# GpSimd asks for pair 1's q, k and v before it sets up constants

## The chip, the cores and the metric

The kernel runs on one core of a Trainium2 chip. A core has engines that run side by side and wait for one another through semaphores: TensorE (PE, with its weight loads shown as PEld), VectorE (DVE), ScalarE (ACT), GpSimd (POOL) and SyncE (SP). Loads and stores are asked for by an engine and carried out by 16 DMA engines. The metric is the device time of one execution in microseconds (us); less is better. Before the change it was 261.1 us, the median of 3 runs (260.87 to 262.47).

## The reference

Linear attention without a softmax, RMS norm over the head dimension, then two matrix products with a gate between them:

```python
kv = np.einsum('bhsd,bhse->bhde', k, v)
out = np.einsum('bhsd,bhde->bhse', q, kv)
rms = np.sqrt(np.mean(out * out, axis=-1, keepdims=True) + 1e-06)
x = out / rms * g_norm          # 8 batches, 8 heads, 576 rows, 64 wide
# x transposed to (8 * 576, 512)
h = x @ w_in                    # 512 -> 2048
g = h * (1.0 / (1.0 + np.exp(-1.702 * h)))
return g @ w_out                # 2048 -> 512
```

All inputs are float32; the kernel computes in float16 with float32 sums.

## The kernel before

Work goes batch by batch: attention of a batch gives `xT` (the transposed, normed rows), and then come the two products with the gate (`Hidden`, `SevenIn`, `Seven`). Attention of the next batch is woven into the products of the present one by lists of steps written out by hand; each engine carries out its instructions in the order in which the program names them. From batch 1 on, that order keeps PE in dense work. Batch 0 has nothing to be woven into and stands alone at the start; the change lies there.

The eight heads of a batch are four **pairs**, numbered 0 to 3. Batch 0 does for each pair `c`:

- `q(c)` (L408): twelve transposes on PE with the identity `ident`, then a copy to `qT` on DVE (L418).
- `kv(c)` (L399): twelve small products of k and v (L249), then on DVE (L402) the copy to `kvb`, multiplied by `ones2`, a 128 x 128 matrix of two 64 x 64 blocks of ones, so that the two heads of a pair don't mix.
- `out(c)` (L282): the product of `kvb` and `qT`, then Square on ACT (L300).
- `ss(c)` (L357): a product with `ones2` that adds up the squares, then the reciprocal root on ACT (L359).
- `apply(c)` (L367): on DVE, the output times the root and `g_col`, written to `xT`.

The pairs are interleaved from L851 on. The order on PE is: twelve `busy` products (512 columns wide, on a zeroed tile, whose results nobody reads), `q(0)`, two more `busy`, `kv(0)`, two small products for `g_col`, two `busy`, `out(0)`, `q(1)`, `kv(1)`, `ss(0)`, `out(1)`, `q(2)`, `kv(2)`, `ss(1)`, `out(2)`, `q(3)`, `kv(3)`, `ss(2)`, the first two products with `w_in` (L451), `out(3)`, further products with `w_in`, and among them `ss(3)`; the products that need `apply(3)` end this part. On DVE, `apply(0)` stands behind the `kvb` copy of pair 2, `apply(1)` between the `qT` copy and the `kvb` copy of pair 3.

Loads of batch 0 come on two queues. SyncE asks for pair 0's k, q and v (L152) in float32, into the staging tile `qf`; DVE and ACT cast them to float16 (L833 to L835). GpSimd asks for q, k and v of pairs 1, 2 and 3 (`early_load`, L90), nine loads, which convert to float16 on the way. The weights follow on GpSimd's queue: seven loads of `w_in` (L171), then `w_out` (L196) and batch 1's q, k, v. Eight semaphores take turns for GpSimd's loads: from the ninth load on, each issue waits for the landing of the load eight places before it.

Before its first load, GpSimd sets up constants. DVE zeroes `ident` (L155) and `kvb[1]` (L156), which the `busy` products read. GpSimd then writes the ones onto the diagonal of `ident` with a select (L157), and fills `ones2` by three memsets (L166 to L168):

```python
nc.gpsimd.memset(ones2, 0.0)
nc.gpsimd.memset(ones2[0:D, 0:D], 1.0)
nc.gpsimd.memset(ones2[D:P, D:P], 1.0)
...
for c in range(1, NPAIR):
    for n in "qkv":
        early_load(n, 0, c, c + 1)
```

Of the kernel before, what the change touches and what calls it, by code (L numbers as in the profile page):

```python
# [9 lines left out]
ALU = mybir.AluOpType  # L10
AFT = mybir.ActivationFunctionType

P = 128
# [3 lines left out]
def kernel(  # L17
# [10 lines left out]
    nc = tc.nc  # L28

    B, H, S, D = q.shape  # L30
# [39 lines left out]
    ident = const.tile([P, P], F16)  # L70
    ones2 = const.tile([P, P], F16)
# [14 lines left out]
    def early_src(n, b, c0, c1):  # L86
        return srcs[n][b, 2 * c0 : 2 * c1].rearrange("h (p j) d -> p h (j d)", j=NJ)

    def early_load(n, b, c0, c1):
        nc.gpsimd.dma_start(  # L90
            out=raw[n][0:PE_, c0:c1, :].rearrange("p c (l x) -> p (c l) x", l=2),
            in_=early_src(n, b, c0, c1),
        )
# [52 lines left out]
    for n in "kqv":  # L146
# [7 lines left out]
    nc.scalar.dma_start(out=g_row, in_=g_norm.unsqueeze(0))  # L154
    nc.vector.memset(ident, 0.0)  # L155
    nc.vector.memset(kvb[1], 0.0)  # L156
    nc.gpsimd.affine_select(  # L157
        out=ident,
        in_=ident,
        compare_op=ALU.not_equal,  # L160
        fill=1.0,
        base=0,
        pattern=[[-1, P]],
        channel_multiplier=1,
    )
    nc.gpsimd.memset(ones2, 0.0)  # L166
    nc.gpsimd.memset(ones2[0:D, 0:D], 1.0)
    nc.gpsimd.memset(ones2[D:P, D:P], 1.0)  # L168

    def load_w_in(f0, f1, k0=0, k1=KO):  # L170
        nc.gpsimd.dma_start(  # L171
            out=w_in_sb[:, k0:k1, f0 * P : f1 * P],
            in_=moe_w_in[k0 * P : k1 * P, f0 * P : f1 * P].rearrange(
                "(ko ki) f -> ki ko f", ki=P
            ),
        )

    for c in range(1, NPAIR):
        for n in "qkv":
            early_load(n, 0, c, c + 1)  # L180
    load_w_in(0, 4, 0, 1)
    load_w_in(0, 4, 1, 2)
    load_w_in(0, 4, 2, KO)
# [887 lines left out]
```

## Time and profile before

| | |
|---|---|
| time, median of 3 runs | 261.1 us (260.87 to 262.47) |
| the profiled execution's own time | 260.98 us |
| its span in the profile | 259.2 us |
| PE busy | 251.8 us (97% of the span) |
| DVE busy | 194.7 us (75%) |
| ACT busy | 174.9 us (67%) |
| POOL busy | 53.6 us (21%) |

Times in the profile count from the start of the span. A timeline row gives start, duration, engine, line, operation, what it writes and reads, how many instructions are merged into it, and in brackets how long the engine sat idle before it and what ended that. "issue" there means that no cause is shown. A row with DMA on POOL or on SPq (SyncE's queue) is the issue of a load, not its transfer. In the view of DMA queues, q0 is GpSimd's queue and q1 SyncE's; a row gives packets, MB, and the time that the packets took as a share of 16 engines over the stretch, which passes 100% where packets of one engine overlap. The chain that ended last is followed back from the last instruction, at each step to whatever released it.

### The profile page before, as it was taken

The numbers are of one execution on the slowest core, as the hardware profiler recorded it, in microseconds if no ns is written. First come the engines' busy times: TensorE is split into PE (matmuls) and PEld (weight loads), VectorE is DVE, ScalarE is ACT, GpSimd is POOL, SyncE is SP. The second block draws the span as 40 slices with busy tenths as digits, with TensorE's granted clock in tenths as the row PEclk, the third lists the DMA queues.
The fourth block names the chain that finished last, engine by engine and source line by source line (L and its number), as shares of the span: only waits on it lengthen the run. The fifth ranks groups of instructions, "written<-read, shape, count | busy, mean of one in ns | idle before, by whom it ended". The sixth has DMA issues, their size and how long they took to land.

```text
span 259.2 us, 6157 instructions
## 1 busy us (share of the span) xinstructions
PE 251.8 (97%) x2500; PEld 206.3 (80%) x2500; DVE 194.7 (75%) x351; ACT 174.9 (67%) x315; POOL 53.6 (21%) x81
## 2 busy tenths in 40 slices
PE   8799999999999999999999999999999999999993
PEld 3444554788888988898889988988899888888882
DVE  1565676899968986898689958995899587557842
ACT  3477725988649964996499648974897569737820
POOL 8862245116034002500160017000000000000001
PEclk9999999999999999999999999999999999999999
DMA  7999999999999946994699799966500710021005
GB/s 174 198 202 206 204 204 196 228 188 146 201 144 193 198 78 163 153 214 71 159 105 230 102 143 157 219 82 158 154 1 12 160 73 3 0 97 68 3 0 162
DMA packets 68558, 35.31 MB, mean 136 GB/s; under 512 B 37874, under 2 KB 65778, under 8 KB 68402
## 3 DMA queue, kind: packets, MB, share of 16 engines
q0 software_dynamic: 37520, 18.17, 54.3%
q1 hardware_dynamic: 30688, 16.36, 27.5%
q8 instruction: 19, 0.31, 0.5%
q10 hardware_dynamic: 322, 0.39, 0.4%
q14 instruction: 9, 0.07, 0.1%
HBM read 36.70 MB, written 9.44 MB: 178 GB/s over the span
## 4 chain that ended last, share of the span: by engine, by line
PE 93%; POOL 2%; DMA 2%; DVE 1%; ACT 0%; issue 0%
PE h L558 38%; PE o L680 38%; PE o L794 5%; PE hT L451 5%; DMA vbuf<-in_v_dram 2%; PE outR L309 2%; PE kvp L237 2%; PE ss L357 1%; POOL qraw L90 1%; POOL kraw L90 1%; POOL vbuf L90 0%; PE kvp L249 0%; PE outT L282 0%; PE q L432 0%; DVE xT L367 0%; PE outT L286 0%
## 5 line engine op out<-in xcount | busy, mean ns | idle before, releaser
L538 ACT ACTIVATE gT<-h 128x512 f16<-128x512 f32 x96 | 52.8, 604 | 5.4 <-PE h L558 5.3
L558 PEld LDWEIGHTS <-ws 128*128 128x128 f16 x512 | 50.1, 98 | 5.8
L680 PEld LDWEIGHTS <-gS 128*128 128x128 f16 x512 | 49.7, 98 | 5.7
L558 PE MATMUL h<-xS,ws 128*128 128x256 f16 x384 | 52.2, 273 | 0.0
L680 PE MATMUL o<-tw,gS 128*128 128x256 f16 x384 | 46.3, 273 | 0.0
L558 PEld LDWEIGHTS <-w_in_sb 128*128 128x128 f16 x384 | 37.1, 98 | 4.7
L680 PEld LDWEIGHTS <-gT 128*128 128x128 f16 x384 | 37.0, 98 | 4.0
L680 PE MATMUL o<-w_out_sb,gT 128*128 128x256 f16 x256 | 33.5, 273 | 0.0
L558 PE MATMUL h<-xT,w_in_sb 128*128 128x256 f16 x224 | 31.9, 273 | 0.0
L655 DVE TENSOR_TENSOR osb<-o,qf 128x512 f32<-128x512 f32 (+1 forms) x25 | 16.7, 668 | 15.1 <-PE o L680 12.3
L572 DVE TENSOR_TENSOR h<-h,s 128x512 f32<-128x512 f32 x32 | 22.2, 697 | 6.8 <-PE h L558 5.5
L574 DVE TENSOR_TENSOR s<-h,s 128x512 f32<-128x512 f32 x32 | 22.1, 691 | 4.1 <-PE h L558 3.3
L114 POOL DMA_DIRECT2D kraw<-in_k_dram x7 | 6.0, 853 | 91.6 <-PE kvp L237 87.2
L610 DVE TENSOR_TENSOR gS<-gT 128x512 f16<-128x512 f16 (+2 forms) x32 | 21.7, 684 | 0.6 <-ACT gT L538 0.6
L538 ACT ACTIVATE gT<-s 128x512 f16<-128x512 f32 x32 | 19.8, 628 | 2.6 <-DVE s L574 2.6
L359 ACT ACTIVATE rs<-ss,eps_t 128x512 f32<-128x512 f32 (+1 forms) x16 | 9.2, 582 | 16.6 <-PE ss L357 16.5
L713 POOL DMA_DIRECT2D out_dram<-osb x2 | 1.1, 562 | 92.4 <-DVE osb L655 92.4
L558 PE MATMUL h<-xS,w_in_sb 128*128 128x256 f16 x128 | 18.9, 273 | 0.0
L966 ACT ACT_TABLE_LOAD x14 | 18.0, 1283 | 0.2
L508 ACT COPY h<-h 128x512 f32<-128x512 f32 x27 | 15.7, 585 | 2.1 <-PE h L558 2.0
L558 PE MATMUL h<-xT,ws 128*128 128x256 f16 x112 | 16.8, 273 | 0.0
L794 PE MATMUL o<-w_out_sb,gT 128*128 128x512 f16 x64 | 16.6, 380 | 0.0
(100 smaller groups left out, 367.8 us busy)
## 6 DMA issues: line engine op xcount, KB each, us to landing
out_dram<-osb SPq DMA_DIRECT2D x10, 512.0 KB, 3.1
kraw<-in_k_dram POOLq DMA_DIRECT2D x5, 512.0 KB, 7.8
vbuf<-in_v_dram POOLq DMA_DIRECT2D x5, 512.0 KB, 11.5
qraw<-in_q_dram POOLq DMA_DIRECT2D x3, 512.0 KB, 13.4
qbuf<-in_q_dram POOLq DMA_DIRECT2D x3, 512.0 KB, 12.7
out_dram<-osb SPq DMA_DIRECT2D x6, 192.0 KB, 6.1
w_in_sb<-in_moe_w_in_dram POOLq DMA_DIRECT2D x2, 512.0 KB, 10.5
w_out_sb<-in_moe_w_out_dram POOLq DMA_DIRECT2D x2, 512.0 KB, 15.1
```

The lines of the kernel that those rows point to most:

```text
L359: nc.scalar.activation(rs[:, 0:n], t[:, 0:n], AFT.Abs_reciprocal_sqrt, bias=eps_t, scale=1.0 / D)
L451: nc.tensor.matmul(self.h[fo], w_in_sb[:, ko, fo * P : (fo + 1) * P], self.x[:, ko], start=(ko == 0), stop=(ko == KO - 1),)
L508: (nc.vector.tensor_copy if engine == "D" else nc.scalar.copy)(to, src)
L538: nc.scalar.activation(self.gT[:, to, n * TH : (n + 1) * TH], src, AFT.Gelu_apprx_sigmoid)
L558: nc.tensor.matmul(bank[name][:, a], w, x, start=(p in (1, 5) and a == 0 and k == 0), stop=(k == KH - 1), skip_group_check=True,)
L572: nc.vector.tensor_add(bank["z"], bank["x"], self.s5)
L574: nc.vector.tensor_add(self.s5, bank["x"], self.s5)
L610: op(s[:, n, lo], a, b)
L655: nc.vector.tensor_add(o, ps, self.kept[with_][:, m])
L680: nc.tensor.matmul(o, a, w, start=(p in (1, 2, 5) and i == 0 and (mo == 0 or split)), stop=(i == HF - 1), skip_group_check=True,)
L794: nc.tensor.matmul(os[mo], gT[:, fo, mo * P : (mo + 1) * P], w_out_sb[:, fo, :], start=(fo == 0), stop=(fo == FO - 1),)
L966: u2.setdefault(i, []).append(lambda: f(*args))
```

## The change

The select on `ident` moves behind pair 1's three loads in GpSimd's program, and the three memsets of `ones2` go from GpSimd to DVE, behind the memset of `kvb[1]`. DVE's instructions are three more and GpSimd's three fewer; the order of everything else is as before on all engines. Nearly all lines behind the changed place stand one line further down in the new kernel (the copy to `kvb` is L403 there instead of L402); the issue of the `w_in` loads is L162 instead of L171 and keeps its place in the order.

```diff
     nc.vector.memset(ident, 0.0)
     nc.vector.memset(kvb[1], 0.0)
-    nc.gpsimd.affine_select(
-        out=ident,
-        in_=ident,
-        compare_op=ALU.not_equal,
-        fill=1.0,
-        base=0,
-        pattern=[[-1, P]],
-        channel_multiplier=1,
-    )
-    nc.gpsimd.memset(ones2, 0.0)
-    nc.gpsimd.memset(ones2[0:D, 0:D], 1.0)
-    nc.gpsimd.memset(ones2[D:P, D:P], 1.0)
+    nc.vector.memset(ones2, 0.0)
+    nc.vector.memset(ones2[0:D, 0:D], 1.0)
+    nc.vector.memset(ones2[D:P, D:P], 1.0)
...
     for c in range(1, NPAIR):
         for n in "qkv":
             early_load(n, 0, c, c + 1)
+        if c == 1:
+            nc.gpsimd.affine_select(
+                out=ident,
+                in_=ident,
+                compare_op=ALU.not_equal,
+                fill=1.0,
+                base=0,
+                pattern=[[-1, P]],
+                channel_multiplier=1,
+            )
```

## The prediction

> **What bounds the kernel now.** I read the busy shares first, then the stretches on either side of 17.15 us, then the chain that ended last, and last the timeline of the first 18 us.
>
> ```profile
> span 259.2 us, 6157 instructions
> PE 251.8 (97%) x2500; PEld 206.3 (80%) x2500; DVE 194.7 (75%) x351; ACT 174.9 (67%) x315; POOL 53.6 (21%) x81
> ```
>
> ```profile
> 17.15:254.95 237.80, 237.78 (x2364) 199.95 (x2363) 187.08 (x331) 167.03 (x305) 38.93 (x53) 1.00 0.81 132
> ```
>
> The second fence is the view by stretches (length, then PE, PEld, DVE, ACT, POOL, then the clock). From 17.15 us on, PE is busy 237.78 of 237.80 us: it waits for nothing. So whatever moves PE's start into that stretch moves the end by the same amount, and nothing after 17.15 us can be won by earlier loads. The profiled execution took 260.98 us, 1.78 us more than its span; the median of the runs shown is 261.1, that is 0.12 higher.
>
> The change lies in the first microseconds. The chain of waits names a load in front of that stretch:
>
> ```profile
> 7.34 5.59 DMA vbuf<-in_v_dram
> ...
> 13.06 0.38 PE kv L249 x12
> ...
> 17.15 4.48 PE hT L451 x20
> ```
>
> This is pair 3's v, the last of the nine loads that GpSimd asks for at L90. It lands at 12.93 (7.34 + 5.59) and PE's `kv(3)` starts at 13.06. The timelines of PE, DVE, GpSimd and SyncE's queue show what stands around it (start, duration, engine, line; in brackets the idle time ahead and its releaser):
>
> ```profile
> 7.60 0.38 PE L249 MATMUL kv<-vbuf,kraw 96*64 96x64 f16 x12 [0.63 <-DVE vbuf L835]
> ...
> 11.95 0.45 PE L412 MATMUL q<-ident,qraw 96*64 96x96 f16 x12
> 13.06 0.38 PE L249 MATMUL kv<-vbuf,kraw 96*64 96x64 f16 x12 [0.67 <-DMA vbuf<-in_v_dram]
> ...
> 13.64 0.61 PE L451 MATMUL hT<-xT,w_in_sb 128*128 128x512 f16 x2
> 14.09 0.38 PE L282 MATMUL outT<-qT,kvb 128*128 128x512 f16 x1
> ```
>
> ```profile
> 6.91 0.64 DVE L835 CAST vbuf<-qf 96x768 f16<-96x768 f32 x1 [2.37 <-DMA qf<-in_v_dram]
> ...
> 12.43 0.46 DVE L418 COPY qT<-q 128x576 f16<-128x576 f16 x1 [0.21 <-PE q L412]
> 12.81 0.74 DVE L367 SCALAR_TENSOR_TENSOR xT<-outT,g_col,rs 128x512 f16<-128x512 f32 x1
> 13.48 0.29 DVE L402 TENSOR_TENSOR kvb<-kv,ones 128x128 f16<-128x128 f32 x1
> ```
>
> ```profile
> 1.02 0.29 POOL L157 TENSOR_SCALAR_AFFINE_SELECT ident<-ident 128x128 f16<-128x128 f16 x1 [0.56 <-DVE ident L155]
> 1.26 0.20 POOL L166 MEMSET ones<- 128x128 f16 x1
> ...
> 1.70 0.15 POOL L168 MEMSET ones<- 64x64 f16 x1
> 1.79 0.78 POOL L90 DMA_DIRECT2D qraw<-in_q_dram  x1
> ```
>
> ```profile
> 0.76 0.41 SPq L152 DMA_DIRECT2D qf<-in_k_dram  x1
> 1.22 0.43 SPq L152 DMA_DIRECT2D qf<-in_q_dram  x1
> 1.70 0.45 SPq L152 DMA_DIRECT2D qf<-in_v_dram  x1
> ```
>
> There are two gates. At 7.60 PE starts `kv(0)`, 0.63 us idle, released by the cast of pair 0's v, which SyncE's queue brought. From there to 12.40 (11.95 + 0.45) runs a chain of latencies through PE, DVE and ACT. At 13.06 comes the second gate, 0.67 us idle, released by GpSimd's last load. But behind it DVE isn't free either: it is in `apply(1)` (L367) from 12.81 to 13.55, and the copy of `kv(3)` (L402) starts at 13.48, as that ends. Were the load earlier, the product behind `kv(3)` would wait for DVE instead of memory.
>
> **The change part by part.**
>
> *GpSimd's work ahead of its first load.* It loses the select and three memsets, which end at 1.85 (1.70 + 0.15). SyncE's first issue stands at 0.76, so the engines are free by then and the first issue moves from 1.79 to about 0.8: 1.0 us earlier. Pair 1's three issues follow; the select (0.29) now stands behind them, so pairs 2 and 3 are asked for about 0.7 earlier. The order of the loads is the same, and no wait on a landing moves to another load. Whatever the last load gains by this is bounded by the queue, not by its issue:
>
> ```profile
> vbuf<-in_v_dram POOLq DMA_DIRECT2D x3, 144.0 KB, 5.4
> ```
>
> Columns: how many, size of one, median us from issue to landing. Nine issues in the 5.55 us from 1.79 to 7.34 are 0.69 apart, and each waits 5.4 for its landing: about eight stand in line. The first lands near 7.2 (1.79 + 5.4), the ninth at 12.93, so one leaves the line each 0.72 us. Bringing requests forward to a line that is already full lands nothing earlier unless the line itself starts earlier.
>
> *Identity and ones.* PE needs `ident` at `q(0)`, which follows twelve warming matmuls; the select would end near 3.4 (0.8, three issues at 0.78 as the row at 1.79 has it, and 0.29). The three memsets on DVE cost at most about 0.5 together by GpSimd's own times (the longest quoted is 0.20), and stand ahead of nothing before the first cast near 4 us; the first reader of `ones2` is L402 after 8 us. The matmuls that warm PE wait only for `kvb[1]`, set before them. Cost: nothing; without that cover, DVE's 0.5 would delay the first cast.
>
> *What the earlier line meets.* Pair 0's k, q, v come on SyncE's queue at the same time; these are the last two:
>
> ```profile
> qf<-in_q_dram SPq DMA_DIRECT2D x1, 288.0 KB, 3.8
> qf<-in_v_dram SPq DMA_DIRECT2D x1, 288.0 KB, 5.2
> ```
>
> The packets by queue (q1 SyncE's, q0 GpSimd's), in 3.5 to 4.5, 4.5 to 5.0, 5.5 to 6.5 and 7.0 to 8.0 us, one fence each:
>
> ```profile
> q1 hardware_dynamic: 173, 0.24, 106.0%
> ```
>
> ```profile
> q1 hardware_dynamic: 75, 0.11, 91.9%
> q0 software_dynamic: 5, 0.00, 14.9%
> ```
>
> ```profile
> q0 software_dynamic: 255, 0.18, 120.1%
> q1 hardware_dynamic: 23, 0.03, 9.9%
> ```
>
> ```profile
> q0 software_dynamic: 276, 0.20, 132.4%
> ```
>
> Alone, SyncE's queue moves 173 packets a us, 10.8 on each of 16 engines: 92 ns each. Alone, GpSimd's moves 276: 58 ns each. GpSimd's first data move between 4.5 and 5.0, 2.7 us or more after the issue at 1.79. Between 5.5 and 6.5 the last 23 packets of SyncE's queue come through among 255 of GpSimd's, and pair 0's v lands only at 6.9 (1.70 + 5.2), 1.9 after q (1.22 + 3.8 = 5.0), though most of its packets were through by 5.5. An engine that serves both in turn gives SyncE's queue one packet per 150 ns (92 + 58).
>
> If GpSimd's data begin 1.0 us earlier, then in that us an engine moves 6.7 of SyncE's packets instead of 10.8. The 4.1 left over come through at 150 ns each: pair 0's v lands **0.62 us later**, at 7.53. Below lies nothing (if GpSimd's data wait until SyncE's queue runs dry), above 1.35 (if they begin 2.2 us earlier: the rival below). I take 0.62, since the mixed stretch in 5.5 to 6.5 is the nearest row.
>
> The Trainium skill's page "DMA: Bandwidth & Descriptors" (section Queues, rings and completion order) says that each DMA engine goes round its queues in turn, a packet block at a time; it speaks against asking early beside a load that is needed first. The mixed 5.5 to 6.5 agrees that neither queue has precedence. With strict halves, a us of earlier sharing would cost v 1.0 us rather than 0.62, and the sum would be 0.4 higher.
>
> *The path.* `kv(0)` moves from 7.60 to 8.22. The chain to the end of `q(3)` carries this along, 12.40 to 13.02; so `kv(3)` finds its v there, and starts at 13.06 as before. The 0.67 of idle time is used up, not won. But DVE carries 0.62 too: its copy at 12.43 goes to 13.05, `apply(1)` ends at 14.17, and the copy of `kv(3)` runs 14.10 to 14.39. `out(3)` can follow at 14.39 instead of 14.09. Before, it could have started at 13.77 (13.48 + 0.29) and stood behind the two products of 13.64; that slack, 0.32, is all that takes up some of the delay. After `out(3)` come Square, `ss(3)`, the root, `apply(3)` and the product at 17.15, one waiting for the other.
>
> Sum: 0.62 − 0.32 = **+0.30 us**, so 260.98 + 0.30 = 261.28 against the profiled run, 261.40 against the median. I give 261.3. A measurement of this kernel can tell about 1%, 2.6 us, from no change: this is well inside.
>
> **The rivals.**
>
> *Nothing moves.* GpSimd's data began at 4.5 to 5.0 just as SyncE's queue ran out; if that was the cause, v still lands at 6.9 and the time is 261.0 to 261.1. For it: only 5 packets before 5.0. Against it: once they came, they went beside SyncE's rather than behind.
>
> *The gain arrives.* If the DMA engines do more with both queues in line (75 + 5 packets in half a us before, 255 + 23 in a whole us after), the ninth load and the first weights land a little earlier. One us at 278 instead of 173 packets would be 105 packets, or 0.38 us at 276 a us. If v of pair 0 isn't late, `kv(3)` starts at 12.68 (13.06 − 0.38), yet `out(3)` still waits for DVE's copy (13.77): the gain is 0.32 at most, 260.7 to 260.9. This is the faster side, and it needs pair 0's v to land no later than 6.9 all the same.
>
> *A longer overlap.* The lag from issue to data isn't fixed. Later in the kernel a load was issued onto an empty queue:
>
> ```profile
> 57.39 0.88 POOL L114 DMA_DIRECT2D kraw<-in_k_dram  x1 [10.93 <-PE kvp L237]
> ```
>
> No packet of GpSimd's queue moved from there to 58.9, and 22 did in 58.9 to 59.4: a lag of 1.5 to 2.0 us:
>
> ```profile
> q0 software_dynamic: 22, 0.01, 82.0%
> ```
>
> With 1.5 after 0.8, data begin at 2.3, some 2.2 us earlier than now. Then 2.2 × 4.1 packets × 150 ns = 1.35 us for v, less 0.32: +1.03, 262.0 to 262.1. The same page of the Trainium skill (section Latency and other measured facts) puts the first byte on GpSimd's path at about 1 us; the 1.9 us or more between the end of the first issue (1.79 + 0.78) and 4.5 are against it here.
>
> *PE falls back to the slow clock.* This is the one case that can be slower by over 1%.
>
> ```profile
> 1.28 4.78 PE L842 MATMUL idle<-kvb 128*128 128x512 f16 x12 [1.28 <-DVE one_t L192]
> ```
>
> These twelve took 0.40 each, the products at 17.15 took 0.22 (4.48/20): PE warms up first. PE would now be idle for up to 1.25 us ahead of `kv(0)` (0.63 + 0.62). Should that send it back for some 4 us, as long as the warming took, the chain's six large products (`out` and `ss` of three pairs) cost 0.18 more each, 1.1 on top of 0.3: 262.4. If it lasts to 17 us, some fourteen more follow (2.5): 264.9. Against it: gaps of 0.63 and 0.67 didn't do it. It decides from the gap at which PE's clock gives way, which no row here shows. The page "TensorE: Matmul & The Clock Gate" of the Trainium skill (Part 1) asks about 3.4 us of idle time for a fall back, by which it stays away.
>
> **How the numbers follow.** Forecast (+0.1 to +0.8): 0.55. Nothing moves: 0.18. The gain arrives: 0.10. Longer overlap: 0.12. Slow clock: 0.05, most of it (0.04) as the long one. The range, 260.7 to 262.3, holds all but the slow clock and the edges of the others, and the scatter of the runs (260.87 to 262.47) lies about as wide. Faster by over 1% would need 2.6 us of a stretch whose stalls are 0.63 + 0.67: 0.01. Slower by over 1%: 0.04. Within: 0.95.
>
> **What would show it.** Right: GpSimd's first issue near 0.8; q0 packets in 3.5 to 4.5; the cast of v at about 7.5 and `kv(0)` at 8.2; `kv(3)` near 13.1 without a wait for memory; the copy of `kv(3)` behind `apply(1)` at about 14.1; the dense stretch at 17.5. Wrong: v's cast at 6.9 (nothing moved) or at 8 and later (longer overlap), or `out(3)` before 14.0 (gain). What would overturn all of it is idle time of PE after 17.5, or slow products between 8 and 16 us.

## The result, and the profile after

The changed kernel takes **262.13 us** (median of 17 executions, 261.29 to 264.84); the kernel before, measured beside it, 261.37 (17 executions, 260.87 to 262.47). The ratio is 1.0039, with a 95% interval of 1.0022 to 1.0056: slower by 0.4%, about 1.0 us in the mean and 0.76 between the medians, where +0.3 was forecast. The time lies inside the stated range; the size was missed.

The page of the changed kernel, its profiled execution 262.16 us long, and the view by stretches from where the dense part now begins:

```profile
span 260.4 us, 6156 instructions
...
PE 251.6 (97%) x2500; PEld 206.2 (79%) x2500; DVE 194.9 (75%) x354; ACT 174.9 (67%) x315; POOL 53.4 (20%) x78
```

```profile
17.95:256.10 238.15, 237.78 (x2364) 199.96 (x2363) 187.09 (x331) 167.01 (x305) 39.06 (x53) 1.00 0.82 131
```

The span grew by 1.2 us (260.4 against 259.2). The dense part begins at 17.95 instead of 17.15, 0.80 later, and holds the same 237.78 us of PE work in 238.15: 0.37 us of it is a new wait. Together that is the 1.2. PE's timeline shows both, and what stands ahead:

```profile
8.65 0.38 PE L250 MATMUL kv<-vbuf,kraw 96*64 96x64 f16 x12 [1.48 <-DVE vbuf L836]
...
13.88 0.38 PE L250 MATMUL kv<-vbuf,kraw 96*64 96x64 f16 x12 [0.46 <-DMA vbuf<-in_v_dram]
14.19 0.39 PE L358 MATMUL ss<-sq,ones 128*128 128x512 f16 x1
14.44 0.60 PE L452 MATMUL hT<-xT,w_in_sb 128*128 128x512 f16 x2
14.88 0.38 PE L283 MATMUL outT<-qT,kvb 128*128 128x512 f16 x1
...
17.95 3.40 PE L452 MATMUL hT<-xT,w_in_sb 128*128 128x512 f16 x15 [0.27 <-DVE xT L368]
...
38.95 0.38 PE L250 MATMUL kvp<-vbuf,kraw 96*64 96x64 f16 x12 [0.37 <-DMA vbuf<-in_v_dram]
```

`kv(0)` starts at 8.65 instead of 7.60, after 1.48 us without work. `kv(3)` still waits for its load and comes at 13.88 instead of 13.06. `out(3)` is at 14.88 (14.09 before), the dense part follows, and at 38.95 PE waits for batch 1's v, for which it didn't wait before. The products are as long as before (0.38 us for `out`): in this execution the clock held. DVE shows where the first delay comes from, and GpSimd how little earlier it asks:

```profile
8.04 0.56 DVE L836 CAST vbuf<-qf 96x768 f16<-96x768 f32 x1 [3.28 <-DMA qf<-in_v_dram]
...
13.83 0.74 DVE L368 SCALAR_TENSOR_TENSOR xT<-outT,g_col,rs 128x512 f16<-128x512 f32 x1
14.49 0.28 DVE L403 TENSOR_TENSOR kvb<-kv,ones 128x128 f16<-128x128 f32 x1
```

```profile
1.32 0.78 POOL L90 DMA_DIRECT2D qraw<-in_q_dram  x1 [0.87 <-POOLq L1056]
...
7.92 0.83 POOL L90 DMA_DIRECT2D vbuf<-in_v_dram  x1 [1.03 <-DMA qraw<-in_q_dram]
```

The first issue moved from 1.79 to 1.32 only; ahead of it GpSimd does nothing for 0.87 us, which its constants had covered before. And the cast of pair 0's v moved from 6.91 to 8.04. The ninth load is asked for at 7.92 (7.34 before), because its issue waits for the landing of the first, which took 6.31 us. The chain that ended last names these loads and then batch 1's v:

```profile
1.32 6.31 DMA qraw<-in_q_dram
12.60 9.38 DMA w_in_sb<-in_moe_w_in_dram
22.56 16.25 DMA vbuf<-in_v_dram
```

Packets by queue from 4.0 to 5.0 us, first before the change, then after it:

```profile
q1 hardware_dynamic: 162, 0.23, 97.0%
q0 software_dynamic: 5, 0.00, 7.4%
```

```profile
q0 software_dynamic: 103, 0.08, 56.5%
q1 hardware_dynamic: 94, 0.12, 49.2%
```

From 5.0 to 6.0 after the change:

```profile
q0 software_dynamic: 107, 0.08, 55.2%
q1 hardware_dynamic: 110, 0.16, 53.4%
```

GpSimd's data now run beside SyncE's from 4.0 on, nearly one packet for one: 210 against 204 in these two us. SyncE's queue, on which pair 0's v stands last, moves 68 packets less in the first of them (94 instead of 162). So more of them are left behind 6.0; from there to 8.0, before the change and after it:

```profile
q1 hardware_dynamic: 11, 0.01, 2.2%
```

```profile
q1 hardware_dynamic: 50, 0.07, 10.6%
```

v's landing takes 6.3 us from the issue (5.2 before):

```profile
qf<-in_v_dram SPq DMA_DIRECT2D x1, 288.0 KB, 6.3
```

One thing stands outside that profile. Each execution comes with the mean clock that TensorE was granted, and five of the changed kernel's 17 had one under 0.995 (0.978 to 0.993); these took 262.96 to 264.84 us. The other twelve had a median of 261.97. The profile shows one of the twelve. The last experiments go after these five.

### The profile page after: what moved, and what is told of

The parts are those of the page before. It is cut to its first block, busy times and chain, and to the rows that moved or that the text cites. A ratio compares the mean times of both kernels' runs of the same rounds, so it can differ in the third digit from the quotient of the medians.

```text
span 260.4 us, 6156 instructions
## 1 busy us (share of the span) xinstructions
PE 251.6 (97%) x2500; PEld 206.2 (79%) x2500; DVE 194.9 (75%) x354; ACT 174.9 (67%) x315; POOL 53.4 (20%) x78
## 4 chain that ended last, share of the span: by engine, by line
PE 83%; DMA 12%; POOL 2%; issue 1%; DVE 0%; POOLq 0%
PE h L559 38%; PE o L681 38%; DMA vbuf<-in_v_dram 6%; DMA w_in_sb<-in_moe_w_in_dram 4%; DMA qraw<-in_q_dram 2%; PE o L795 2%; PE outR L310 2%; PE kvp L238 2%; POOL w_in_sb L162 1%; PE ss L358 1%; PE kvp L250 1%; PE outT L283 0%; POOL vbuf L90 0%; PE outT L287 0%; DVE osb L659 0%
```

## The experiments

Three questions: is the early issue the cause, or the new place of the select and the memsets? What decides whether GpSimd's data get in beside v? And what lowers the clock in some executions? Letters A, B and C of an expectation hold for the runs of its own group. Tiles named `pause` and `late` are read by nobody. "Clock low" means a mean granted clock under 0.995 in an execution.

### Is it the early issue?

**Both edits kept, GpSimd's first load held back** by five memsets:

```diff
+    for _ in range(5):
+        nc.gpsimd.memset(pause, 0.0)
     for c in range(1, NPAIR):
```

> The changed kernel, with five memsets of an unused 128 x 128 tile on GpSimd ahead of its first load, so that this is issued near 1.8 us again (1.79 before, 1.32 after the change); the select stays behind pair 1's loads and ones2 on DVE. Theory (the earlier start of GpSimd's loads costs the time): the cast of pair 0's v back at 6.9 to 7.1 (8.04 after the change), the dense stretch of PE from about 17.2, time 261.1 to 261.5. Rival (the select between the loads, or the memsets on DVE, cost it): v's cast stays near 8.0, time 262.0 to 262.3.

Measured: 261.32 us (260.83 to 262.95), ratio 0.9996 (0.9976 to 1.0015). GpSimd's first issue and DVE's cast of v in its trace:

```profile
1.94 0.78 POOL L91 DMA_DIRECT2D qraw<-in_q_dram  x1
```

```profile
6.87 0.56 DVE L839 CAST vbuf<-qf 96x768 f16<-96x768 f32 x1 [2.00 <-DMA qf<-in_v_dram]
```

The loss is gone with select and memsets at their new places. Those places cost nothing that can be measured here; the early load does.

**One half of the change at a time.** First only the ones go to DVE:

```diff
-    nc.gpsimd.memset(ones2, 0.0)
-    nc.gpsimd.memset(ones2[0:D, 0:D], 1.0)
-    nc.gpsimd.memset(ones2[D:P, D:P], 1.0)
+    nc.vector.memset(ones2, 0.0)
+    nc.vector.memset(ones2[0:D, 0:D], 1.0)
+    nc.vector.memset(ones2[D:P, D:P], 1.0)
```

> The kernel before, with only the three memsets of ones2 moved to DVE; the select stays ahead of the loads. It ends at 1.31, so the first load should be issued at 1.3 to 1.4. Theory (start of the loads): as after the change, v's cast near 8.0 and 262.0 to 262.3. Rival (the select between the loads): as before the change, 261.2 to 261.5.

Then only the select goes behind pair 1's loads:

```diff
-    nc.gpsimd.affine_select(
-        out=ident,
...
     nc.gpsimd.memset(ones2, 0.0)
...
+        if c == 1:
+            nc.gpsimd.affine_select(
+                out=ident,
...
```

> The kernel before, with only the select moved behind pair 1's loads; the memsets of ones2 stay on GpSimd ahead of the loads, and needn't wait for DVE now. First issue near 1.3 to 1.4, since it can't come before 1.32. Theory: v's cast near 8.0, 262.0 to 262.3. Rival (memsets on DVE): 261.2 to 261.5.

Measured: 261.38 us (ratio 0.9999, 0.9983 to 1.0015) and 261.31 (0.9993, 0.9977 to 1.0009). The issues moved to 1.50 and 1.42, yet v's cast came at 7.13 and 7.31, not at 8. Both expectations missed: neither half costs anything measurable, and the loss doesn't grow in step with an earlier issue.

**The kernel before, GpSimd's first load later:**

```diff
+    for _ in range(3):
+        nc.gpsimd.memset(pause, 0.0)
     for c in range(1, NPAIR):
```

> The kernel before, with three more memsets of an unused tile on GpSimd ahead of its first load: first issue near 2.4 instead of 1.79. Theory: pair 0's v lands earlier by up to 0.9 us (its cast near 6.0 to 6.4 instead of 6.91), as SyncE's queue is nearly through when GpSimd's data begin. If the queue then loses no throughput to mixing, pair 3's v lands no later than 13.0 and the time is 260.9 to 261.3; if the line of nine loads simply starts 0.6 later, kv(3) waits until 13.6 and the time is 261.6 to 262.0. Rival (position of the select or memsets): no change from 261.4.

Measured: 262.21 us (260.92 to 263.96), ratio 1.0033 (1.0003 to 1.0063). With the issue at 2.58, v's cast came at 6.70, but `kv(2)` and `kv(3)` waited 0.59 and 0.64 us for their loads. Seven executions at full clock had a median of 261.21, five with a low clock took 263.25 to 263.96; these carry the median above both forecasts (261.3 and 262.0 at most). So later is no gain either, and here the low clock came without a late v.

### What decides whether the data get in?

**A tiny memset ahead of the first load:**

```diff
+    nc.gpsimd.memset(pause[:, 0:2], 0.0)
     for c in range(1, NPAIR):
```

> The changed kernel with one memset of two columns on GpSimd ahead of its first load; the load should still be issued at 1.3 to 1.35 us, as the changed kernel's 1.32 seems to be set by start-up. Theory A (how early GpSimd's loads are issued against SyncE's v at 1.69 decides): GpSimd's data begin near 4.0 to 4.1, v's cast near 8.0, time 262.0 to 262.3. Rival B (what matters is that a load is GpSimd's very first instruction): data begin near 5.0, v's cast near 7.0, time 261.2 to 261.5.

Measured: 261.58 us (260.94 to 261.81), ratio 1.0002 (0.9985 to 1.0018). Issue and cast:

```profile
1.36 0.78 POOL L91 DMA_DIRECT2D qraw<-in_q_dram  x1 [0.52 <-issue]
```

```profile
7.11 0.56 DVE L838 CAST vbuf<-qf 96x768 f16<-96x768 f32 x1 [2.32 <-DMA qf<-in_v_dram]
```

With an issue 0.04 us later than in the changed kernel, v comes 0.9 earlier. The median still lies 0.42 us over that of the kernel before at full clock on the same chip (261.16); in this trace PE waits 0.61 us for weights at 16.61. Either the load must be GpSimd's first instruction to do harm, or there is a sharp edge between 1.32 and 1.36.

**Pair 0's v on ScalarE's queue,** in the changed kernel and in the one before:

```diff
-        nc.sync.dma_start(out=dst, in_=src)
+        (nc.scalar if n == "v" else nc.sync).dma_start(out=dst, in_=src)
```

> The changed kernel, with pair 0's v asked for by ACT (ahead of g) instead of third on SyncE's queue: its issue moves from 1.69 to about 0.75 us, ahead of GpSimd's first at 1.32. Theory A (the order of arrival decides who waits): v's cast at 5.5 to 6.5 instead of 8.04, the second stall near 38.9 us gone, time 260.8 to 261.4. Rival C (each engine serves all queues in halves from the moment that GpSimd's data are there, whoever came first): with three queues v's cast stays at 7 or later and the time at 261.8 or more.

> The kernel before, with pair 0's v asked for by ACT instead of third on SyncE's queue. All three loads of pair 0 then run beside each other, so k and q land somewhat later and v earlier: v's cast at 5.5 to 6.5 instead of 6.91. kv(3) still waits for pair 3's v (13.06) and out(3) for DVE, so that at most 0.3 us are won: 261.0 to 261.3. If the time falls by more, the wait for pair 3's v was not the second gate.

Measured: 261.56 us (ratio 1.0008, 0.9987 to 1.0029) and 261.53 (1.0008, 0.9993 to 1.0024). In the first, v's cast comes at 5.33, and `kv(0)` and `kv(3)` start at 8.02 and 12.64:

```profile
8.02 0.38 PE L250 MATMUL kv<-vbuf,kraw 96*64 96x64 f16 x12
...
12.64 0.38 PE L250 MATMUL kv<-vbuf,kraw 96*64 96x64 f16 x12
```

With the early issue kept (1.32) and v out of SyncE's line, the ratio can't be told from 1. That fits v's lateness as the cost, but doesn't show that it is the whole: the interval reaches 1.0029 and overlaps the changed kernel's (from 1.0022), the full-clock median is still 0.39 us over that of the kernel before beside it (261.55 against 261.16), and 261.56 lies between the two forecasts. In this trace q is late instead (PE idles 1.72 us ahead of `q(0)`), and PE waits 0.77 us for weights at 16.91. The kernel before gained nothing by the same edit, against the expectation; its q was then the late one, and `kv(0)` came at 8.27.

**Batch 1's kv(0) and kv(1) two steps later** in the changed kernel:

```diff
-                at2((36, 37, 49, 50)[c], of(1, "kv", c))
+                at2((38, 39, 49, 50)[c], of(1, "kv", c))
-                at2((41, 43, 54, 55)[c], of(1, "out", c))
+                at2((43, 45, 54, 55)[c], of(1, "out", c))
-                at2((45, 50, 58, 60)[c], of(1, "ss", c))
+                at2((47, 52, 58, 60)[c], of(1, "ss", c))
-                at2((48, 52, 58, 62)[c], of(1, "apply", c))
+                at2((50, 54, 58, 62)[c], of(1, "apply", c))
```

> The changed kernel, with batch 1's kv(0) and kv(1) two products later in the list (steps 38 and 39 instead of 36 and 37) and its out, ss and apply of pairs 0 and 1 two later as well, so that PE has some 0.43 us of other products ahead of the wait for batch 1's v. If that wait (0.44 us at 38.5 us in the profile of the change) is part of the loss, it goes to 0 to 0.1 and the time falls by 0.3 to 0.45, to 261.7 to 261.9. If it only stands in for a wait further on, the time stays at 262.1 to 262.2.

Measured: 261.93 us (261.41 to 264.92), ratio 1.003 (1.0006 to 1.0055). The trace has no wait near 39 us; v's cast is at 7.79. The ratio stands 0.0009 (0.2 us) under the changed kernel's, with intervals that overlap: the stall at 38.95 is at most a small part of the loss.

**Three runs tell order of arrival from first instruction.** In the kernel before, SyncE's loads are held back by two small ones:

```diff
+    nc.sync.dma_start(out=late[:, 0, :], in_=g_norm.unsqueeze(0))
+    nc.sync.dma_start(out=late[:, 1, :], in_=g_norm.unsqueeze(0))
     for n in "kqv":
```

> Two small SyncE loads stand ahead of pair 0's k, q and v, so these three are issued about 0.9 us later (v at 2.6 instead of 1.70), while GpSimd's constants and its first issue at 1.79 stay as before. Theory A (what counts is whether GpSimd's first load is ahead of SyncE's v by enough: 0.38 us in the changed kernel, 0.34 in the one with the tiny memset, 0.8 here): GpSimd's data move beside q and v from about 4.0 to 4.5, the two queues share one for one, and v's cast comes at 8.8 or later; the time is 262.2 to 263.0. Theory B (what counts is that a load is GpSimd's very first instruction): GpSimd's data come only as v runs out, v's cast is 0.9 later than before, 7.7 to 7.9, and the time is 261.5 to 262.0.

In the changed kernel, GpSimd's first load waits for DVE:

```diff
     nc.vector.memset(ones2[D:P, D:P], 1.0)
+    nc.vector.memset(qraw[0:PE_, 1, :], 0.0)
```

> The changed kernel, but the tile of GpSimd's first load is first zeroed by VectorE behind the ones, so that a load is still GpSimd's first instruction, yet is issued only at about 1.7 to 2.2. Theory A (order of arrival against SyncE's v): the load is no longer ahead, GpSimd's bulk starts near 5.0, v's cast stands at 6.9 to 7.2, and the time is 261.1 to 261.6. Theory B (a load as GpSimd's first instruction): data in 4.0 to 4.5 beside SyncE's, v's cast at 7.7 or later, 261.9 to 262.4.

In the kernel with the tiny memset, SyncE's loads are held back. The expectation speaks of two small loads; the kernel has one, so SyncE's issues stand at 1.16, 1.57 and 2.06 and not where the text puts them:

```diff
+    nc.sync.dma_start(out=late, in_=g_norm.unsqueeze(0))
     for n in "kqv":
...
+    nc.gpsimd.memset(pause[:, 0:2], 0.0)
```

> The changed kernel with one 128x2 memset ahead of GpSimd's first load (issue at 1.36, as in the run with the tiny memset, which lost nothing) and two small SyncE loads ahead of pair 0's k, q and v, whose issues move from 0.75, 1.21 and 1.69 to about 1.6, 2.1 and 2.6. Theory A: GpSimd's load is now ahead of all three, its data move from about 4.0 beside k, q and v, v's cast comes at 9.0 or later, and the time is 262.5 to 263.5. Theory B: as with the tiny memset alone, only 0.9 later: v's cast at 7.9 to 8.1, and the time 261.6 to 262.2.

Measured: 263.1 us (262.06 to 265.06; ratio 1.0079, 1.0045 to 1.0113), 261.63 (260.91 to 263.57; 1.0023, 0.9999 to 1.0047) and 261.59 (261.07 to 264.77; 1.0031, 1.0002 to 1.0059). The cast of v in the three traces, in this order:

```profile
8.12 0.56 DVE L839 CAST vbuf<-qf 96x768 f16<-96x768 f32 x1 [2.63 <-DMA qf<-in_v_dram]
```

```profile
6.45 0.56 DVE L837 CAST vbuf<-qf 96x768 f16<-96x768 f32 x1 [1.53 <-DMA qf<-in_v_dram]
```

```profile
8.33 0.56 DVE L840 CAST vbuf<-qf 96x768 f16<-96x768 f32 x1 [3.39 <-DMA qf<-in_v_dram]
```

B falls twice. A load that is GpSimd's first instruction does no harm when it is issued at 2.46; one behind a memset lets v be cast at 8.33 instead of 7.11 when SyncE asks 0.37 later: 0.85 beyond its own later request. A has the direction right, though its sizes were too large (8.8 and 9.0 expected, 8.12 and 8.33 measured), and the third time, 261.59, is nearer to B's (261.6 to 262.2). The first kernel's loads were profiled once more, with more products on PE (under *The clock*), and there v came earlier:

```profile
7.77 0.56 DVE L839 CAST vbuf<-qf 96x768 f16<-96x768 f32 x1 [2.28 <-DMA qf<-in_v_dram]
```

That is only 0.23 beyond its own later request, and by the cast alone it is what B had forecast (7.7 to 7.9). How far GpSimd's first issue lies ahead of SyncE's issue of v, and when v is cast:

| | ahead by, us | v's cast, us |
|---|---|---|
| before, paused | −0.89 | 6.70 |
| first load waits for DVE | −0.77 | 6.45 |
| changed kernel, paused | −0.25 | 6.87 |
| before | −0.09 | 6.91 |
| ones only | 0.19 | 7.13 |
| select only | 0.28 | 7.31 |
| tiny memset | 0.33 | 7.11 |
| changed kernel, the same again, the same with more products | 0.37, 0.37, 0.36 | 8.04, 7.54, 8.24 |
| batch 1's kv later | 0.36 | 7.79 |
| before, SyncE held back, and with more products | 0.54, 0.54 | 8.12, 7.77 (v asked for 0.63 later) |
| tiny memset, SyncE held back | 0.70 | 8.33 (0.37 later) |

Up to 0.33 us v loses 0.4 at most; from 0.36 on it loses 0.6 to 1.3 where SyncE's own issues are unmoved. Casts with the same start scatter by 0.7, so they alone wouldn't show an edge. The packets do: from 4.0 to 4.5 us GpSimd's queue moved none or one in each run with a lead of up to 0.33, and 46 to 69 in the four with 0.36 or 0.37. In the two traces with SyncE held back it moved 57 and 82 from 4.5 to 5.0, against 5 in the kernel before, although SyncE's data came later there; so the load that cost v only 0.23 had come in early too, against B. And with v on ScalarE's queue, asked for before it, the load that is GpSimd's first instruction moved none before 4.5. The order of arrival decides when GpSimd's data begin; what that costs v differs from execution to execution. What makes so sharp an edge no run shows. The run with the load that waits for DVE has the earliest v of all, and is no faster: `kv(2)` and `kv(3)` there wait 1.31 and 0.63 us for their own loads. The gates stand close together, and whichever load is favoured, another one is late.

### The clock

Sorting all executions by clock gave this:

| | executions | clock low | median of the rest, us |
|---|---|---|---|
| before, beside the experiments | 121 | 9 | 261.23 |
| changed kernel, both runs | 29 | 10 | 261.85 |
| before, SyncE held back | 7 | 5 | 262.12 |

The profile of the held-back kernel is of an execution with a low clock (264.91 us), and shows where it fell. Columns as in the view by stretches, the clock third from the end:

```profile
5.20:8.60 3.40, 1.78 (x18) 0.67 (x17) 0.77 (x2) 0.83 (x1) 2.42 (x4) 1.00 1.22 221
8.60:8.70 0.10, 0.00 (x0) 0.00 (x0) 0.10 (x2) 0.00 (x0) 0.01 (x1) 0.91 1.40 207
8.70:18.80 10.10, 10.06 (x103) 5.02 (x103) 4.78 (x12) 4.23 (x7) 7.75 (x11) 0.50 1.32 199
18.80:19.00 0.20, 0.20 (x2) 0.13 (x1) 0.00 (x0) 0.00 (x0) 0.00 (x0) 0.70 1.23 202
```

At about 8.7 us the granted clock drops to 0.50 and stays there for 10.2 us. Ahead of it PE was busy for 1.78 of 3.40 us, with two gaps of 0.88. Most falls must be shorter: seven of the changed kernel's ten low executions have a mean clock of 0.992 or 0.993, two 0.977 or 0.978. Executions at full clock read 0.996 to 1.000; so at half clock the seven stand for some 2 to 4 us and the two for some 9 to 12, an estimate from these means and the span.

If the gaps are the cause, filling them with the warming products cures it. The changed kernel, with four more products in its longer gap:

```diff
     a0.q(0)
-    busy(2)
+    busy(6)
     a0.kv(0)
```

> The changed kernel with six warming products instead of two between q(0) and kv(0); nothing else moves, and kv(0) still starts at 8.6 to 8.7. If part of the loss is the clock (5 of the changed kernel's 17 executions had a mean granted clock under 0.995 and took 263.0 to 264.8, against 7 of 92 of the kernel before), and PE's idle 1.48 us ahead of kv(0) is what brings it down, then at most 1 in 16 executions has a clock under 0.995, the median is 261.9 to 262.0, and no execution is over 262.4. If the clock falls for another reason, 4 or 5 of 16 stay low and the median is 262.1.

The held-back kernel, with three more in each of its gaps:

```diff
-    busy(12)
+    busy(15)
     a0.q(0)
-    busy(2)
+    busy(5)
     a0.kv(0)
```

> The kernel before with two small SyncE loads ahead (5 of 7 executions had a clock under 0.995, median 263.1; PE sat idle 0.88 us ahead of q(0) and 0.88 ahead of kv(0)), now with three more warming products ahead of each of the two, so that both gaps shrink to 0.2 or 0.3. If idle time brings the clock down: at most 1 of 7 is low, products between 9 and 18 us take 0.38 each and not 0.6, the median is 262.0 to 262.3. If not: 4 or 5 of 7 are low and the median stays near 263.

And the changed kernel once more beside them:

> The changed kernel itself once more, beside the run with the gap filled: median 262.0 to 262.2, executions at full clock near 261.9, and 3 to 6 of 16 with a mean clock under 0.995. Its trace shows again the first issue at 1.32, GpSimd's data from about 4.0, v's cast near 8.0, and the wait for batch 1's v near 39 us.

Measured, on one chip: 261.72 us (261.26 to 262.84, ratio 1.0007, 0.9987 to 1.0027), **none of 12** low; 262.06 (261.9 to 262.61, 1.0026, 1.0013 to 1.004), **none of 10** low; and the changed kernel 262.17 (261.57 to 264.77, 1.0042, 1.0019 to 1.0064), 5 of 12 low, the other seven at a median of 261.74. So the added products win back the low executions and no more: 261.72 is the changed kernel's time at full clock. PE of the held-back kernel without gaps, then of the changed kernel with four more products, whose v came at 8.24 in this trace, so that a gap was left:

```profile
8.51 0.38 PE L253 MATMUL kv<-vbuf,kraw 96*64 96x64 f16 x12
```

```profile
8.93 0.38 PE L250 MATMUL kv<-vbuf,kraw 96*64 96x64 f16 x12 [1.10 <-DVE vbuf L836]
```

`kv(0)` takes 0.38 us in both, 0.53 at half clock. Against 5 of 7, none of 10; against 10 of 29, none of 12: chance alone would give the first 3 times in 1000, the second 18 in 1000 (Fisher's exact test, one-sided; the 5 of 7 are from another chip). So more work on PE in these microseconds keeps the clock up. Which property of the idle time decides isn't shown, and the longest gap isn't it: the changed kernel's first profile has 1.48 us and PE busy for 1.69 of 3.40 us (5.2 to 8.6) at full clock, and the kernel with four more products kept 1.10. With v on ScalarE's queue PE idles 1.72 us in the trace, and 2 of 12 executions are low; the kernel before with a later first load has 0.92 in its trace, and 5 of 12. The first median, 261.72, lies under its forecast (261.9 to 262.0), and the 262.4 us that no execution of it was to pass was passed by one, at 262.84 and full clock.

The repeat of the changed kernel missed two of its forecasts, v's cast near 8.0 and the wait near 39 us; the profile of the result isn't the only course at full clock:

```profile
7.54 0.56 DVE L836 CAST vbuf<-qf 96x768 f16<-96x768 f32 x1 [2.79 <-DMA qf<-in_v_dram]
```

```profile
8.15 0.38 PE L250 MATMUL kv<-vbuf,kraw 96*64 96x64 f16 x12 [0.66 <-DVE vbuf L836]
...
15.68 0.59 PE L452 MATMUL hT<-xT,w_in_sb 128*128 128x512 f16 x2
16.89 4.27 PE L452 MATMUL hT<-xT,w_in_sb 128*128 128x512 f16 x19 [0.62 <-DMA w_in_sb<-in_moe_w_in_dram]
```

Here v is 0.63 late and `kv(0)` 0.55, yet the span is 259.9, 0.7 over before. PE stops at 16.89 for the weights: four products that ran ahead of the wait before the change (0.87 us, from x6 in 1.46 against x2 in 0.59) now stand behind it, so 16.89 + 0.87 = 17.76 answers to 17.15, +0.61. Nothing waits at 39 us. v is late in both profiles; behind it one waits for batch 1's v (span 1.2 over before), the other for the weights (0.7 over).

No kernel of these is faster than the one before.

## Why the prediction was wrong

It named the right mechanism and mis-sized it. In the profile of the result, 0.80 us of PE's later start stand where the sum had 0.30, because v lost 1.13 instead of 0.62, and 0.37 us of a wait stand where it had nothing. And it put a further cost, the clock, down as a rival that won't happen.

*First issue near 0.8.* It moved to 1.32. The step took GpSimd to be free when SyncE is; the 0.87 us without work ahead of a first load wasn't in the trace of before, where the constants covered it.

*GpSimd's data 1.0 us earlier, v 0.62 later.* **This is the term that failed.** The data did come about 1.0 earlier (4.0 against 5.0), though the issue moved by 0.47: the link between the two is an edge, not a fixed lag, and the forecast of this step came true by luck. Then v lost 0.63, 0.88, 1.13 and 1.33 in four traces with this start: all within the stated bounds of nothing and 1.35, but the value taken lies at their lower end. For the first us the working was right: 4.1 packets on each of 16 engines are 66, and SyncE's queue moved 66 to 74 less from 4.0 to 5.0 in the four traces. What it missed is the end. Behind 6.0 the queue had 31, 32, 50 and 51 packets left, in the order of v's casts, against 11 before, and v lands with the last one. In the profile of the result 32 packets were missing already between 2.5 and 4.0 (297 against 329); why, and why the end differs so, stays open. The page "DMA: Bandwidth & Descriptors" of the Trainium skill (section Queues, rings and completion order) has the engines go round their queues in turn; 210 against 204 packets agree, and its strict halves, 1.0 us, were nearer to three of the four traces than the 0.62 taken; for the first us alone halves would be 81 packets (half of 162), and the 66 of the working fit better.

*The line is full, so the ninth load lands at 12.93 as before.* It failed too. The ninth issue waits for the first landing, and that came about 0.4 later (1.32 + 6.31 = 7.63, against the 7.2 that the prediction worked out). `kv(3)` waited 0.46 for memory, where the prediction had the wait used up. It cost nothing in this trace: `kv(3)` was done at 14.26, and DVE was in `apply(1)` until 14.57. Sharing costs both queues.

*DVE behind `kv(3)`, slack 0.32.* Right: the copy stands behind `apply(1)` (13.83 + 0.74, copy at 14.49), and 1.05 at `kv(0)` became 0.80 at the dense part.

*Nothing after 17.15 can wait.* It held for earlier loads, and was used for later ones: GpSimd's queue fell behind, and batch 1's v (asked for at 22.56, 0.37 us of wait in one trace) or the weights (0.62 in the other) became late. "What would overturn all of it" named this.

*Identity and ones cost nothing.* Right, by the paused kernel.

*The slow clock, chance 0.05.* It was priced as a yes or no for the kernel, decided by the length of the gap. It is a matter of executions: 10 of 29 against 9 of 121. Nor does the clock column show the warming that the rival started from: it reads 1.00 from 1 to 6 us of the kernel before, where the twelve products take 0.40 each. The mean of all executions rose by 1.03 (262.43 against 261.39), the full-clock median by 0.62 (261.85 against 261.23); so some 0.4 of the 1.0 is the clock (an estimate), and the rest goes with the earlier load at full clock. The page "TensorE: Matmul & The Clock Gate" of the Trainium skill (Part 1), by which it should have stayed away, asks for an idle window of about 3.4 us. The trace at half clock had none: its longest gap between products was 0.88 us. There the measurement decides. But the page also says that the window runs free of the kernel, and 10.2 us at half clock is three of them; a window that starts anywhere would explain why the same kernel falls in some executions only. That part is argued, not shown.

## What to carry to other kernels

Two loads on different queues shared the engines nearly packet for packet here (210 against 204), so an early request for what is needed later is paid by what is needed first: look at which landing opens the first gate before asking for anything sooner. Where a kernel's start is a chain of waits, put products that nobody reads into TensorE's idle time: its cost isn't only its length, but also the executions in which the clock falls (none of 22 with such products added, 15 of 36 without). And where times scatter, sort the executions by granted clock before explaining a median with a profile of one.

## What the runs showed of the hardware

- Where a load stands first and waits for no other engine, it is issued at 1.32 or 1.33 us in all five runs, after 0.87 or 0.88 us without work; a 128 x 2 memset ahead of it costs 0.04.
- Between an issue 0.33 and 0.36 us ahead of SyncE's v, the start of GpSimd's data jumps: with SyncE's own issues in place, none or one of its packets moves from 4.0 to 4.5 us up to 0.33, and 46 to 69 do at 0.36 and 0.37. The cause stays open.
- While the queues share, they move no more together than one alone: 0.20 and 0.24 MB in the us from 4.0 and from 5.0, against 0.24 of SyncE's queue (3.5 to 4.5, before) and 0.20 of GpSimd's (7.0 to 8.0, before). In packets it is 197 and 217 against 173 and 276, as GpSimd's are smaller.
- Gaps of 0.88 us, twice in 2.7 us, were followed by 10.2 us at half clock, and that execution's span is 2.7 us over those of the full-clock executions of the same kernel (263.1 against 260.4 and 260.3).
